# First layer: four of the six pieces of the attention's weights split ahead of the fourth chunk's inverse products, three staging buffers

## The chip, the cores and the metric

The kernel runs on one core of a Trainium2 chip. The metric is the device time of one execution in microseconds (us), lower is better. Before the change the median of 3 runs is 3002.05 us (3000.38 to 3004.14).

The engines have short names in what follows: PE multiplies matrices (PEld is its loading of weights), DVE and ACT work on vectors and single elements, POOL fills memory and issues one queue of transfers, SP issues another. Each engine takes its own instructions strictly one after another and waits for others by semaphores.

## The reference

Four layers, each added to its own input after a layer norm: a long convolution (a state space model computed by FFT), an attention with one key and value head for 32 query heads, and the same two again with the same weights. `x` is 2048 x 640.

```python
def _A_ref(u, ...):                     # convolution layer
    P = jnp.exp(logdA[:, :, None] * l[None, None, :])
    K = jnp.einsum("dn,dnl,dn->dl", Cc, P, dB).real
    Kf = rfft(pad(K)); Uf = rfft(pad(u))
    y = irfft(Uf * Kf)[..., :L]
    return y + u * Dskip

def _B_ref(x, wq, wk, wv, wo):          # attention layer
    q, k, v = x @ wq, x @ wk, x @ wv
    p = softmax(q k^T * Dh ** -0.5)
    return (p v) @ wo

x = x + _A_ref(_layernorm(x), ...)      # layer a
x = x + _B_ref(_layernorm(x), ...)      # layer b
x = x + _A_ref(_layernorm(x), ...)      # layer c
x = x + _B_ref(_layernorm(x), ...)      # layer d
```

## The kernel before

**The program.** First the convolution's kernels are generated, then come the layers a (convolution), b (attention), c (convolution), d (attention). The attention layers take most of the time. The change touches the end of layer a.

**A convolution layer** works in five chunks of 128 channels, `c` = 0 to 4. A chunk goes through these steps: the normalised input `xn` is multiplied on PE with a table `wf` (tiles `za`, L652) and ACT copies the result to a spectrum `A` (L654); DVE finishes the forward transform with short butterflies (`fft8`, L114 and L117); DVE multiplies with the spectrum of the kernel, `kh`, which SP loads (2 MB, L762, tile `Akh`); DVE does the inverse butterflies; PE multiplies with the table `wi` (`inverse`, L853 and L860, tiles `ya`) in four groups of four time steps each, and the result goes back into `x` (`residual`: by ACT on L869 for the fourth chunk, by DVE on L871 for the third and the fifth). For chunks 0 to 3 two of the products' sums are made by transfers that POOL issues and that add into `Aa` while they move (`spread`, L923 and L927). For the fifth chunk all of it is done on DVE (`product`, L837, and `fft8_last`, L157 and L160). Two banks of PSUM hold the groups of `ya` in turn, so the third group of a chunk can begin when the residual of the first has been read out.

**Statistics.** The layer norm of the attention that follows needs sums over each row of `x`. While the fourth chunk is prepared, ACT sums the channels 0 to 383, which are final by then, in four groups (`stats_first`, L692, L694, L696: four sums, one shift, four sums of squares, each writing what it doesn't need to a `dump` buffer). DVE then makes `base` of all sixteen sums of squares (`stats_base`, L701), which it needs much later.

**The attention's weights.** The attention multiplies in a format with fewer bits, in three products of high and low parts, so its weights are split once, in layer a, into `wh` (high) and `wl` (low), `attn_weights`. There are six pieces: piece 0 is `kv`, the narrow `wv` and `wk` side by side (five blocks of 20 columns each, loaded on L1017 and L1018), and pieces 1 to 5 are the five row blocks of `wq` (128 x 640 each, loaded on L1031). `first(k)` rounds a piece on ACT (L1036, into `wh`) and subtracts on PE (`ident` times the piece, L1038, plus `minus` times its high part, L1040, tile `pw`); `second(k)` copies the difference on ACT to `wl` (L1045). `scr`, the tile `xnas`, takes the place of `xn` once the fifth chunk's `za` has read it; it holds the staged row blocks, the `dump` buffers and `minus`. At the end both parts are also written to memory (`whd`, `wld`), and layer c only loads them back.

**The order.** PE, ACT and DVE follow the order in which the code is written, except that independent small instructions of DVE are moved among each other by the builder of the program; SP's and POOL's queues follow a scheduler. In the last chunk a helper, `weave`, places calls between DVE's instructions: `late` is a list of (position, call). Before the change it holds the four residuals of the fourth chunk (`turn`) and all twelve halves of the six pieces.

Of the kernel before, what the change touches and what calls it, by code (L numbers as in the profile page):

```python
# [23 lines left out]
D = 640  # L24
# [7 lines left out]
NA = D - 2 * DC  # L32
# [151 lines left out]
def weave(calls, between):  # L184

    for i in range(len(calls) + 1):
        for n, call in between:
            if n == i or (i == len(calls) and n > i):
                call()
        if i < len(calls):  # L190
            calls[i]()


class Net:
# [595 lines left out]
    def conv_layer(self, nm, first):  # L790
# [7 lines left out]
        with tc.manual_schedule(engines={mybir.EngineType.PE, mybir.EngineType.Activation,  # L798
# [29 lines left out]
            def new_xn(c):  # L828
                if "xn" in self.placed:
                    return self.placed.pop("xn")  # L830
                return cv.tile([P, 24, DC], F32, tag="xn", bufs=1, name=f"xn{nm}{c}")
# [4 lines left out]
            def product(A, kh):  # L836
                return [lambda a=a: tt(*a) for a in (  # L837
                    (m(B, 0), m(A, 0), m(kh, 0), ALU.mult),
                    (R, m(A, 1), m(kh, 1), ALU.mult),
                    (m(B, 0), m(B, 0), R, ALU.subtract),  # L840
                    (m(B, 1), m(A, 0), m(kh, 1), ALU.mult),
                    (R, m(A, 1), m(kh, 0), ALU.mult),
                    (m(B, 1), m(B, 1), R, ALU.add))]
# [22 lines left out]
            def residual(c, g, y):  # L866
                y = y.rearrange("p (t d) -> p t d", t=4)
                if c in (0, NCH - 2):
                    nc.scalar.activation(stream(c, g), y, AF.Copy)  # L869
                else:  # L870
                    tt(stream(c, g), y, stream(c, g), ALU.add)  # L871
                if c == NCH - 1:
                    self.stats_last(g)
# [65 lines left out]
            for c in range(NCH):  # L939
                A = As.pop(c)  # L940
                if c == NCH - 1:
                    late = [(1, lambda turn=turn: turn(0)), (2, lambda turn=turn: turn(1)),
                            (4, lambda turn=turn: turn(2)), (5, lambda turn=turn: turn(3))]
                    late = sorted(late + [(3 + k, a[0]) for k, a in enumerate(pieces)]
                                  + [(5 + k, a[1]) for k, a in enumerate(pieces)], key=lambda a: a[0])
                    K = khs.pop(c)
                    weave(product(A, K) + fft8_last(nc, A, B, R, K), late)
                else:
                    spread(A, khs.pop(c))
                    khs[c + 1] = self.load_spectrum(c + 1)  # L950
                    woven = [] if turn is None else [
                        (n, lambda turn=turn, g=g: turn(g)) for g, n in enumerate((2, 6, 10, 14))]
                    N = As[c + 1]
                    weave(self.whole(N, -1) if c + 1 < halved else fft8(nc, N, B, -1), woven)
                    if c + 2 < NCH:
                        As[c + 2] = prepare(c + 2)
                    if c + 2 == NCH - 1:
                        self.wfs.pop().close()
                    if c == NCH - 2:
                        scr = new_xn("s").rearrange("p a d -> p (a d)")  # L960

                        def dump(n):
                            return scr[:, 1280 + NA * (n % 4) : 1280 + NA * (n % 4) + NA]

                        self.stats_setup(nm)
                        for g in range(4):
                            self.stats_first(g, dump)
                        pieces = self.attn_weights(scr, nm == "a")
                    weave(self.whole(A, +1), ())
                ys = [inverse(c, g, K if c == NCH - 1 else A) for g in range(2)]  # L970

                def turn(g, c=c, A=A, ys=ys):

                    residual(c, g, ys[g])
                    if g < 2:
                        ys.append(inverse(c, g + 2, A))
# [24 lines left out]
    def attn_weights(self, scr, fresh):  # L1001


        nc, ins = self.nc, self.ins
        stack = ExitStack()
        wp = stack.enter_context(self.tc.tile_pool(name="wqp", bufs=1, side="right", reuse_waits="tile"))
        wh = wp.tile([P, 5, 692], F32R, name="wh")
        wl = wp.tile([P, 5, 692], F32R, name="wl")
        self.wqs = stack, wh, wl
        parts = [(w.bitcast(F32), dst) for w, dst in ((wh, self.whd), (wl, self.wld))]  # L1010
        if not fresh:
            for w, dst in parts:
                nc.sync.dma_start(w, dst.rearrange("p (k n) -> p k n", k=5))
            return []
        kv = wp.tile([P, 5, 52], F32, name="kv")
        nc.gpsimd.memset(kv, 0.0)
        nc.sync.dma_start(kv[:, :, 0:20], ins["B_wv"].rearrange("(k p) n -> p k n", p=P))  # L1017
        nc.sync.dma_start(kv[:, :, 32:52], ins["B_wk"].rearrange("(k p) n -> p k n", p=P))  # L1018
        minus = scr[:, 2816:2944]
        nc.scalar.activation(minus, self.ident, AF.Copy, scale=-1.0)  # L1020
        pws = {}

        def ends(k):
            return (wh[:, k - 1, 0:D], wl[:, k - 1, 0:D]) if k else (wh[:, :, D:692], wl[:, :, D:692])

        def first(k):
            hi = ends(k)[0]
            pw = pws[k] = self.ps2(f"pw{k}")
            if k:
                src = scr[:, D * (k % 2) : D * (k % 2) + D]  # L1030
                nc.sync.dma_start(src, ins["B_wq"][P * (k - 1) : P * k])  # L1031
                cuts = [(pw[:, a:b], src[:, a:b], hi[:, a:b]) for a, b in ((0, 512), (512, D))]
            else:
                src = kv
                cuts = [(pw[:, 0:260].rearrange("p (k n) -> p k n", k=5), src, hi)]
            nc.scalar.activation(hi, src, AF.Copy)  # L1036
            for o, a, _ in cuts:
                nc.tensor.matmul(o, self.ident, a, start=True, stop=False)  # L1038
            for o, _, b in cuts:
                nc.tensor.matmul(o, minus, b.bitcast(F32), start=False, stop=True)  # L1040

        def second(k):
            pw = pws.pop(k)
            src = pw[:, 0:D] if k else pw[:, 0:260].rearrange("p (k n) -> p k n", k=5)
            nc.scalar.activation(ends(k)[1], src, AF.Copy)  # L1045
            if k == 5:
                for w, dst in parts:
                    nc.sync.dma_start(dst.rearrange("p (k n) -> p k n", k=5), w)

        return [(lambda k=k: first(k), lambda k=k: second(k)) for k in range(6)]  # L1050

    def attn_layer(self, nm, out=None):
# [415 lines left out]
```

## Time and profile before

| what | value |
|---|---|
| median of 3 runs | 3002.05 us |
| the profiled execution's own time | 2999.59 us |
| its span, first to last instruction | 2997.8 us |
| mean granted clock of PE over the span | 0.956 |
| PE busy | 93% of the span |
| ACT busy | 81% of the span |
| DVE busy | 46% of the span |
| end of layer a, from the fifth chunk's last `za` to the attention's first product | 539.3 to 620.3 us |

The times in the rows of the trace are microseconds from the start of the span. In the view in order of time the columns are the start, the time until the group's end, the engine, the line, the operation, output and inputs, shapes, the count, and in brackets how long the engine sat idle before it and what ended that. SPq and POOLq rows are the issue of a transfer, not its landing. In the transfers' view a queue's row has packets, MB and the share of 16 transfer engines' time in the stretch asked for; q1 is the queue of SP, q0 that of POOL. In the view by stretches a row has the stretch, its length, the busy time of PE, PEld, DVE, ACT and POOL with counts, PE's granted clock (1.00 is full), the transfer engines' share and GB/s. Some of the instructions of the program appear as two in the trace of PE: one product of `inverse` is two there.

### The profile page before, as it was taken

Reading aid. Unit: us, or ns where it says so; the run is one execution under the profiler, and the core shown is the slowest. Engines: PE = TensorE matmul, PEld = TensorE weight load, DVE = VectorE, ACT = ScalarE, POOL = GpSimd, SP = SyncE. Lnnn points to the kernel's source line nnn. Section 1 sums busy time; section 2 is a strip of 40 time slices with the busy share of each in tenths; the row PEclk is TensorE's granted clock in tenths of the full one; section 3 lists DMA queues with packets and bytes.
Section 4 is the critical chain, followed back from the end, with each engine's and each line's share of the span. In section 5 each row is a group of like instructions: output and inputs, shape, how many; then the busy total and the mean of one; then the engine's idle time right before and its main releaser. Section 6 shows DMA issues by size and latency. Waiting matters only on the chain. (4 is left out here: it accounts for less than half of the span.)

```text
span 2997.8 us, 52536 instructions
## 1 busy us (share of the span) xinstructions
PE 2777.6 (93%) x21712; PEld 1269.2 (42%) x21712; DVE 1378.1 (46%) x1794; ACT 2426.4 (81%) x2904; POOL 86.7 (3%) x149
## 2 busy tenths in 40 slices
PE   2776989898999999999999998898999999999999
PEld 0333978775232333232333687772233333333333
DVE  7999899942122332322232599722222322222222
ACT  5888243444999999999999634338999999999997
POOL 0001001000000000000000011000000000000000
PEclk9855999999999999999999999899999999999999
DMA  6113555433200000001000256131001101110100
GB/s 145 34 19 100 186 162 113 104 114 113 81 22 25 22 25 22 27 21 28 21 26 20 87 113 160 39 129 51 22 25 26 39 21 28 38 26 24 41 19 23
DMA packets 126000, 175.60 MB, mean 59 GB/s; under 512 B 59460, under 2 KB 81988, under 8 KB 122132
## 3 DMA queue, kind: packets, MB, share of 16 engines
q1 hardware_dynamic: 102680, 137.70, 15.8%
q0 software_dynamic: 21104, 33.45, 5.5%
q8 instruction: 175, 2.87, 0.4%
q10 hardware_dynamic: 1968, 0.98, 0.1%
q14 instruction: 73, 0.60, 0.1%
HBM read 95.22 MB, written 48.04 MB: 48 GB/s over the span
## 5 line engine op out<-in xcount | busy, mean ns | idle before, releaser
L1264 ACT ACTIVATE pt<-scb 128x1024 f32<-128x1024 f32 x1024 | 942.2, 1113 | 6.7 <-PE scb L1260 5.1
L1264 ACT ACTIVATE pt<-scd 128x1024 f32<-128x1024 f32 x1024 | 942.1, 1115 | 5.8 <-DMA qpd<-mxd 3.9
L1274 PE MATMUL pob<-pt,vt 128*32 128x512 f32 x4096 | 546.6, 606 | 4.4 <-DVE on L1291 0.2
L1274 PE MATMUL pod<-pt,vt 128*32 128x512 f32 x4096 | 546.3, 605 | 4.4 <-DVE on L1291 0.2
L1260 PE MATMUL scb<-qpb,kt 62*128 62x512 f32 x2048 | 385.8, 451 | 6.0 <-DVEq L1209 5.6
L1260 PE MATMUL scd<-qpd,kt 62*128 62x512 f32 x2048 | 385.4, 451 | 5.6 <-DVEq L1209 5.2
L1260 PEld LDWEIGHTS scb<-qpb,kt 62*128 62x128 f32 x2048 | 166.0, 185 | 401.4 <-ACT pt L1264 392.0
L1260 PEld LDWEIGHTS scd<-qpd,kt 62*128 62x128 f32 x2048 | 165.8, 184 | 401.1 <-ACT pt L1264 392.2
L1322 DVE TENSOR_TENSOR x<-pyd,x 128x320 f32<-128x320 f32 x146 | 71.8, 491 | 560.9 <-PE pyd L1334 560.9
L1322 DVE TENSOR_TENSOR x<-pyb,x 128x320 f32<-128x320 f32 x146 | 71.8, 492 | 547.4 <-PE pyb L1334 547.4
L1294 DVE RECIPROCAL rc<-rc 128x512 f32<-128x512 f32 x62 | 207.9, 3353 | 2.1
L1274 PEld LDWEIGHTS pob<-pt,vt 128*32 128x32 f32 x4096 | 80.6, 108 | 178.1 <-issue 160.0
L1274 PEld LDWEIGHTS pod<-pt,vt 128*32 128x32 f32 x4096 | 80.6, 108 | 177.6 <-issue 159.5
L1334 PE MATMUL pyb<-wo,ot 128*32 128x320 f32 x1168 | 105.3, 432 | 0.0
L1334 PE MATMUL pyd<-wo,ot 128*32 128x320 f32 x1168 | 105.3, 432 | 0.0
L652 PE MATMUL za<-xna,wf 128*128 128x256 f32 x384 | 87.4, 390 | 5.0 <-ACT xna L818 5.0
L652 PE MATMUL zc<-xnc,wf 128*128 128x256 f32 x384 | 85.8, 385 | 5.0 <-ACT xnc L818 5.0
L860 PE MATMUL ya<-Aa,wi 128*128 128x128 f32 x576 | 71.8, 289 | 15.5 <-DVE Aa L114 15.5
L1291 DVE COPY on<-pod 128x512 f32<-128x512 f32 x31 | 21.4, 691 | 134.6 <-PE pod L1274 120.6
L1291 DVE COPY on<-pob 128x512 f32<-128x512 f32 x31 | 21.4, 691 | 133.0 <-PE pob L1274 110.0
L443 PE MATMUL pe<-kg,tm 48*128 48x512 bf16 (+1 forms) x120 | 60.1, 603 | 23.9 <-ACT m L451 15.4
L652 PEld LDWEIGHTS za<-xna,wf 128*128 128x128 f32 x384 | 74.8, 196 | 16.8 <-ACT xna L818 6.2
(367 smaller groups left out, 3204.2 us busy)
## 6 DMA issues: line engine op xcount, KB each, us to landing
Akh<-kh SPq DMA_DIRECT2D x10, 2048.0 KB
kh<-Ak SPq DMA_DIRECT2D x5, 2048.0 KB
qhd<-qh SPq DMA_DIRECT2D x40, 256.0 KB
qld<-ql SPq DMA_DIRECT2D x40, 256.0 KB
qpb<-qhd SPq DMA_DIRECT2D x256, 40.0 KB
qpd<-qhd SPq DMA_DIRECT2D x256, 40.0 KB
ot<-on SPq DMA_DIRECT2D x216, 40.0 KB
wf<-in_c_wf POOLq DMA_DIRECT2D x16, 512.0 KB, 7.9
```

Of the source, the lines that this page charges most:

```text
L443: nc.tensor.matmul(pe[:, 512 * h : 512 * h + 512], grp(tm, u, par, rows), kg[0:rows, col : col + 512], start=True, stop=True)
L652: nc.tensor.matmul(zv[:, :, c, kk], self.wf[:, t + 4 * h, j, c, kk], x, start=(n == 0), stop=(n == 3))
L860: nc.tensor.matmul(y[:, s * DC : (s + 1) * DC], self.wi[:, t, j, c_, kk], v[:, 2 * t + c_, kk], start=(i == 0 and not whole), stop=(i == 3 ...
L1260: nc.tensor.matmul(sc[:, 512 * par : 512 * par + 512], kt[rows, 128 * t : 128 * t + 128], qps[nb, hg, pr][rows], start=True, stop=True)
L1264: nc.scalar.activation(pt, sc, AF.Exp, scale=SCALE)
L1274: nc.tensor.matmul(po[32 * j : 32 * j + 32], vt[:, t], pts[step, j // 2][:, 512 * (j % 2) : 512 * (j % 2) + 512], start=(t == 0), stop=(t ...
L1291: nc.vector.tensor_copy(on, po)
L1294: nc.vector.reciprocal(rc, rc)
L1322: nc.vector.tensor_tensor(xh, py, xh, ALU.add)
L1334: nc.tensor.matmul(py[j : j + m], o[:, 128 * i + j : 128 * i + j + m], w[:, 320 * half : 320 * half + 320], start=start, stop=stop)
```

## The change

Four of the six pieces are begun ahead of the statistics of the fourth chunk instead of being woven into the fifth: `first` of pieces 0 to 3 stands before `stats_first(0)`, `second(0)` after `stats_first(1)`, `second(1)` after `stats_first(2)`, `second(2)` and `second(3)` after `stats_first(3)`. Pieces 4 and 5 stay in the fifth chunk, behind its residuals. The staged row blocks get three buffers in place of two, the `dump` buffers two in place of four, and `minus` moves. The program of layer c has the same two `dump` buffers, and nothing else of the change.

```diff
@@ -941,8 +941,8 @@
                 if c == NCH - 1:
                     late = [(1, lambda turn=turn: turn(0)), (2, lambda turn=turn: turn(1)),
                             (4, lambda turn=turn: turn(2)), (5, lambda turn=turn: turn(3))]
-                    late = sorted(late + [(3 + k, a[0]) for k, a in enumerate(pieces)]
-                                  + [(5 + k, a[1]) for k, a in enumerate(pieces)], key=lambda a: a[0])
+                    late = sorted(late + [(6 + k, a[0]) for k, a in enumerate(pieces[4:])]
+                                  + [(8 + k, a[1]) for k, a in enumerate(pieces[4:])], key=lambda a: a[0])
                     K = khs.pop(c)
                     weave(product(A, K) + fft8_last(nc, A, B, R, K), late)
                 else:
@@ -960,12 +960,16 @@
                         scr = new_xn("s").rearrange("p a d -> p (a d)")
 
                         def dump(n):
-                            return scr[:, 1280 + NA * (n % 4) : 1280 + NA * (n % 4) + NA]
+                            return scr[:, 1920 + NA * (n % 2) : 1920 + NA * (n % 2) + NA]
 
                         self.stats_setup(nm)
+                        pieces = self.attn_weights(scr, first)
+                        for a in pieces[:4]:
+                            a[0]()
                         for g in range(4):
                             self.stats_first(g, dump)
-                        pieces = self.attn_weights(scr, nm == "a")
+                            for a in pieces[max(g - 1, 0) : (0, 1, 2, 4)[g]]:
+                                a[1]()
                     weave(self.whole(A, +1), ())
                 ys = [inverse(c, g, K if c == NCH - 1 else A) for g in range(2)]
 
@@ -1016,7 +1020,7 @@
         nc.gpsimd.memset(kv, 0.0)
         nc.sync.dma_start(kv[:, :, 0:20], ins["B_wv"].rearrange("(k p) n -> p k n", p=P))
         nc.sync.dma_start(kv[:, :, 32:52], ins["B_wk"].rearrange("(k p) n -> p k n", p=P))
-        minus = scr[:, 2816:2944]
+        minus = scr[:, 2688:2816]
         nc.scalar.activation(minus, self.ident, AF.Copy, scale=-1.0)
         pws = {}
 
@@ -1027,7 +1031,7 @@
             hi = ends(k)[0]
             pw = pws[k] = self.ps2(f"pw{k}")
             if k:
-                src = scr[:, D * (k % 2) : D * (k % 2) + D]
+                src = scr[:, D * (k % 3) : D * (k % 3) + D]
                 nc.sync.dma_start(src, ins["B_wq"][P * (k - 1) : P * k])
                 cuts = [(pw[:, a:b], src[:, a:b], hi[:, a:b]) for a, b in ((0, 512), (512, D))]
             else:
```

Behind the inserted code the lines of the changed kernel are higher by 4: L1036 is L1040 there. Three places of the engines' orders matter below.

ACT, after its last copy of the fifth chunk's `za`: a row with + stands there now, the others stood there before (`wh` is the high part, `xnas` the staged row blocks, `L692` the first statistics).

```order
 L654 ACTIVATE Aa_3955<-za_2_3992 128x2x512
 L654 ACTIVATE Aa_3955<-za_3_4010 128x2x512
+L1024 ACTIVATE xnas<-ident 128x128
+L1040 ACTIVATE wh<-kv 128x5x52
+L1040 ACTIVATE wh<-xnas 128x640 x3
 L692 ACTIVATE xnas,smsuma<-x 128x384 x4
 L694 ACTIVATE smshifta<-smsuma 128x4
```

So `minus` and the rounding of four pieces now stand ahead of the first statistics, and what they wait for the statistics wait for too.

DVE, in the inverse butterflies of the fourth chunk (`Aa_3737`): a row with - stood there before, with + it stands there now.

```order
 L114 TENSOR_TENSOR Aa_3737<-B 128x512 x2
-L701 TENSOR_SCALAR smbasea<-smsqa 128x16
 L114 TENSOR_TENSOR B<-Aa_3737 128x512 x2
 L114 TENSOR_TENSOR Aa_3737<-B 128x2x256 x2
 L114 TENSOR_TENSOR B<-B 128x2x256 x2
+L701 TENSOR_SCALAR smbasea<-smsqa 128x16
 L117 SCALAR_TENSOR_TENSOR Aa_3737<-B 128x512 x2
 L117 SCALAR_TENSOR_TENSOR Aa_3737<-B 128x2x256 x2
```

`stats_base`, which reads the sums of squares of all four groups, moves back by six instructions, but it still stands ahead of the last butterflies of the fourth chunk and of everything of the fifth.

SP, in the queue of the changed kernel from the load of the fourth chunk's kernel spectrum (`Akh_3874`) to that of the whole split weights.

```order
L762 DMA Akh_3874<-kh 128x4096
L1035 DMA xnas<-in_B_wq 128x640 x2
L1021 DMA kv<-in_B_wv 128x5x20
L1022 DMA kv<-in_B_wk 128x5x20
L1035 DMA xnas<-in_B_wq 128x640
L762 DMA Akh_4093<-kh 128x4096
L1035 DMA xnas<-in_B_wq 128x640 x2
L1052 DMA whd<-wh 128x3460
```

One load of a row block has moved from behind the fifth chunk's spectrum (`Akh_4093`), where three stood, to ahead of it; the two loads of `kv` stand where they stood.

## The prediction

> **What bounds the kernel now.** I read the page first, then the trace from 539 to 620 us in order of time, engine by engine, because the edit lies inside layer a alone; the attention layers, most of the time, only shift with it. On PE:
>
> ```profile
> 564.58 6.76 PE L860 MATMUL ya<-Aa,wi 128*128 128x128 f32 x32 [9.98 <-DVE Aa L114]
> ...
> 580.90 3.73 PE L860 MATMUL ya<-Aa,wi 128*128 128x128 f32 x32
> 584.47 0.60 PE L1038 MATMUL pw<-kv,ident 128*128 128x260 f32 x2
> ...
> 591.91 1.25 PE L1038 MATMUL pw<-xnas,ident 128*128 128x512 f32 x4
> ...
> 596.30 7.31 PE L860 MATMUL ya<-Akh,wi 128*128 128x128 f32 x64
> 603.45 7.31 PE L860 MATMUL ya<-Aa,wi 128*128 128x128 f32 x64
> ...
> 620.26 0.43 PE L1131 MATMUL pqb<-xh,wh 128*52 128x512 f32 x1 [1.35 <-DVE xl L999]
> ```
>
> From 564.58 to 610.76 (603.45 + 7.31) only the first row has an idle time: PE never stops. It does the fourth chunk's four groups, from 584.47 to 596.3 all six pieces, then the fifth chunk's four groups. Ahead of that it stood idle for 9.98 us, which the change wants to fill. DVE over the same time:
>
> ```profile
> 565.05 0.17 DVE L701 TENSOR_SCALAR smbasea<-smsqa 128x16 f32<-128x16 f32 x1
> 565.16 1.29 DVE L114 TENSOR_TENSOR B<-Aa 128x512 f32<-128x512 f32 x2
> ...
> 568.89 2.50 DVE L117 SCALAR_TENSOR_TENSOR Aa<-B 128x512 f32<-128x512 f32 x4
> 571.43 2.29 DVE L837 TENSOR_TENSOR B<-Aa,Akh 128x2048 f32<-128x2048 f32 x1
> ...
> 589.61 2.49 DVE L157 TENSOR_TENSOR Akh<-Ra 128x512 f32<-128x512 f32 x4
> ```
>
> No row has an idle time: DVE is a chain without gaps. Its first quarter of the output that the fifth chunk's first group reads is ready at 589.61 + 0.62 = 590.2, but PE takes it up at 596.30. So over the last stretch the six pieces on PE decide, by 6.1 us; before it, DVE does. Both bounds lie close together, so a gain on PE is capped by DVE.
>
> **What the removal is worth.** Four pieces leave the tail: from 584.47 to 591.91 is 7.44 us of PE, about 2.2 for a wide piece. DVE's cap makes it less, and layer c shows the capped case: the same chain with no pieces.
>
> ```profile
> 1876.83 2.29 DVE L837 TENSOR_TENSOR B<-Ac,Akh 128x2048 f32<-128x2048 f32 x1
> ...
> 1904.71 2.48 DVE L160 SCALAR_TENSOR_TENSOR Ac<-B 128x512 f32<-128x512 f32 x4
> ```
> ```profile
> 1895.81 10.30 PE L860 MATMUL yc<-Akh,wi 128*128 128x128 f32 x64 [6.49 <-issue]
> 1905.94 7.31 PE L860 MATMUL yc<-Ac,wi 128*128 128x128 f32 x64
> ...
> 1923.07 0.43 PE L1131 MATMUL pqd<-xh,wh 128*52 128x512 f32 x1 [1.09 <-DVE xl L999]
> ```
>
> From DVE's first fifth-chunk product to the attention's first product layer c takes 1923.07 - 1876.83 = 46.24 us, layer a 620.26 - 571.43 = 48.83. The removal is worth 2.6 us, not 7.4. Part of what is lost is PE's clock: the 64 instructions take 10.30 us there against 7.31, after 6.49 us of idling.
>
> ```profile
> 1892.00:1895.00 3.00, 0.00 (x0) 0.00 (x0) 2.97 (x3) 0.00 (x0) 0.00 (x0) 0.50 0.00 0
> ```
>
> The clock column stands at half here, 2.7 us into that gap. In the changed kernel my estimate of the gap is 4.4 us (below), so I take layer c's number. If PE stayed at full clock, the second half could begin when DVE's first L160 result is there (1904.71 + 0.62 = 1905.33 instead of 1905.94), some 0.6 to 0.9 us earlier with DVE's own wait for PE gone: the removal is worth 2.6 to 3.5. [...]
>
> **What the new place costs.** ACT before:
>
> ```profile
> 543.85 0.52 ACT L692 ACTIVATE xnas<-x 128x384 f32<-128x384 f32 x1 [3.33 <-DVE x L871]
> ...
> 562.96 0.19 ACT L696 ACTIVATION_READ_ACCUMULATOR xnas<-x,smshifta 128x1 f32 x1
> 563.06 0.29 ACT L1020 ACTIVATE xnas<-ident 128x128 f32<-128x128 f32 x1
> ```
>
> The statistics take 563.06 - 543.85 = 19.2 us of ACT without a gap and end 1.9 us ahead of L701, the one DVE instruction that reads them all. Now the rounding of pieces 0 to 3 stands ahead of them, and its first piece is `kv`. When does `kv` land? Nobody waited for it before, so I read SP's queue and the bytes, q1 in 544 to 548 us and in 548 to 553.5 us, then both queues in 549 to 550:
>
> ```profile
> 539.53 1.44 SPq L1031 DMA_DIRECT2D xnas<-in_B_wq  x2
> 541.22 1.31 SPq L1017 DMA_DIRECT2D kv<-in_B_wv  x1
> 542.58 1.87 SPq L1018 DMA_DIRECT2D kv<-in_B_wk  x1
> 553.54 0.34 SPq L762 DMA_DIRECT2D Akh<-kh  x1
> ```
> ```profile
> q1 hardware_dynamic: 278, 0.64, 45.8%
> ```
> ```profile
> q1 hardware_dynamic: 1322, 0.12, 30.6%
> ```
> ```profile
> q0 software_dynamic: 189, 0.19, 116.0%
> q1 hardware_dynamic: 190, 0.02, 30.2%
> ```
>
> The first 0.64 MB are the two row blocks (2 x 320 KB). The next 1322 packets with 0.12 MB can only be `kv`: 2 x 128 x 5 = 1280 rows of 80 bytes. They crawl, taking turns packet for packet (190 against 189) with POOL's adding transfers, and the last of them moves in the quarter of a microsecond from 553.25:
>
> ```profile
> q1 hardware_dynamic: 12, 0.00, 3.5%
> ```
>
> What lies between data and use I take from the first late row block: its issue, its last data (q1 in the tenth of a microsecond from 589.1), its use on ACT.
>
> ```profile
> 586.65 4.73 SPq L1031 DMA_DIRECT2D xnas<-in_B_wq  x3
> ```
> ```profile
> q1 hardware_dynamic: 2, 0.00, 1.1%
> ```
> ```profile
> 576.30 0.41 ACT L1036 ACTIVATE wh<-kv 128x260 fp32r<-128x260 f32 x1
> ...
> 585.16 0.73 ACT L1036 ACTIVATE wh<-xnas 128x640 fp32r<-128x640 f32 x1
> 585.79 0.38 ACT L1045 ACTIVATE wl<-pw 128x260 fp32r<-128x260 f32 x1
> ...
> 589.56 0.74 ACT L1036 ACTIVATE wh<-xnas 128x640 fp32r<-128x640 f32 x1 [3.39 <-DMA xnas<-in_B_wq]
> ...
> 594.60 1.28 ACT L1045 ACTIVATE wl<-pw 128x640 fp32r<-128x640 f32 x2
> ```
>
> From 589.1 to 589.56 are 0.4 us. So ACT rounds `kv` at 553.4 + 0.4 = 553.8. Start to start `kv` takes 0.31 us (0.41 less the overlap of 0.1) and a row block 0.63 (585.16 to 585.79): 0.3 + 3 x 0.63 = 2.2. The statistics begin at 556.0, not 543.85.
>
> The third row block, now third in the queue behind `kv`, is needed at 555.3. It must follow `kv` on the transfer engines. At best it costs nothing; at worst it takes, from 553.4 on, all that the late row block took from issue (586.65) to use, 2.9 us, and lands 1.0 late. I take 0, since its issue is long past and only about 1.5 us of moving is left, and keep 1.0 for the range. `minus` (0.29) fits into the wait.
>
> From 556.0 the statistics run 19.2 us, with `second(0)` (0.28) and `second(1)` (0.59, half of 1.28 less the overlap) between them; PE has both differences by 558, long before ACT asks. End: 556.0 + 19.2 + 0.9 = 576.1, with the last read-out 576.2. DVE comes to L701 in its new place at 568.89 - 0.11 = 568.8. **It waits 7.4 us there.** Behind L701 are queued the last butterflies of the fourth chunk and the whole fifth chunk, all that PE waits for at the end. Before, this wait was zero with 1.9 us to spare.
>
> The other edits cost nothing as long as that wait covers them. PE's fourth difference needs a tile that `second(0)` frees at 565.9, and at half clock it takes twice 2.2 us, to 570.3; the fourth chunk's first group then ends near 575.5. The four residuals on ACT follow the statistics and `second(2)`, `second(3)` from 577.3. PE's groups and the last two pieces (2 x 2.2) end near 593.2; DVE's first output comes at 590.2 + 7.4 = 597.6, which is the gap of 4.4 us. The spectrum of the fifth chunk, issued at 553.54, follows 320 KB that now move first, about 1 us; it is used at 578.8. Two `dump` buffers in place of four: a write waits for the write two before it on its own engine, which has ended; nothing (rival B prices the other case). Layer c: nothing.
>
> **The sum**, on the profiled execution: 2999.59 + 7.4 (DVE waits) - 2.6 (pieces out of the tail) = 3004.4. The median of the runs shown lies 2.46 above that execution, so 3002.05 + 4.8 = **3006.9 us**.
>
> **The rivals.**
>
> A, the forecast. Bounds from its own terms: 7.4 to 8.4 for the wait, 2.6 to 3.5 for the gain, so +3.9 to +5.8; with the scatter of the runs (3000.38 to 3004.14, 2 us to either side of the median) +2 to +8.
>
> B, the wait is longer still, because each statistic waits for the one just before it to write its `dump` buffer.
>
> ```profile
> 545.38 0.51 ACT L692 ACTIVATE xnas<-x 128x384 f32<-128x384 f32 x1
> 545.80 0.19 ACT L692 ACTIVATION_READ_ACCUMULATOR xnas<-x 128x1 f32 x1
> 546.02 0.20 ACT L694 ACTIVATE smshifta<-smsuma 128x4 f32<-128x4 f32 x1
> ```
>
> L694 waits for the sum before it and starts 0.64 after that sum's start, where sums follow one another by 0.5. For the 24 statistics that aren't first of their four, 24 x 0.14 = 3.4 more: +8.2, 3010.2. Against it: two buffers call for the write two back only.
>
> C, the other side: `kv` lands early and nothing is slower. It would take that its 1280 rows don't wait for POOL's transfers. If they need only their own share (30.6% of 5.5 us = 1.7), they are done by 549.7, the wait shrinks by 3.7 and the sum is +1.1, 3003.2. For the wait to vanish, `kv` must be usable by 553.8 - 7.4 = 546.4; then only the gain stays: 2999.5 on the median. For it: `kv` is issued by 544.45, and a late block took 2.9 us from issue to use. Against it: the counted packets of this very stretch, with the same queues ahead. [...]
>
> D, PE's chain becomes late. Its groups wait for the residuals, which now stand behind the statistics; if half clock lasted through all four groups (3.7 us each at full), 4 x 3.7 = 15 us more would put PE's last piece at 608, 10 past DVE's output, and the sum at +15. The point from which it decides is 4.4 us of lateness. Against it: in this place before only the first group ran slow, 6.76 us for 32 instructions against 3.73 later. I price the likely partial case at +4 on top, +8.8, 3010.9.
>
> **How the numbers follow.** About 0.2% (6.0 us) is what a measurement of this kernel can tell from no change. A 0.62, of which 0.25 above +6.0 (late third block, scatter) and 0.37 below; B 0.18; D 0.09; C 0.11, of which 0.03 beyond -6.0 with scatter. Slower 0.25 + 0.18 + 0.09 = 0.52, same 0.37 + 0.08 = 0.45, faster 0.03. Range: from A's lower end less the better part of C's first case, 3002.0, to past B and D, 3011.5.
>
> **What would show it.** Right: ACT's first `wh` row waits until near 553.8 for `kv`; the first L692 near 556; L701 with an idle time of some 7 us put down to ACT; the first L837 near 578.8; PE idle 4 to 5 us ahead of `ya<-Akh`, and half clock behind it; the attention's first product near 625. Wrong: an L692 before 550, or L701 with no idle time (C), sums 0.64 apart (B), or `ya<-Akh` starting directly behind the pieces (D). An unchanged stretch of 46.2 us from L837 on with another total would mean the time went elsewhere.

## The result, and the profile after

| what | before | changed |
|---|---|---|
| median, beside each other (14 runs each) | 3001.10 us (2997.40 to 3004.14) | 3008.73 us (3004.84 to 3009.79) |
| ratio of the times, 95% interval | 1 | 1.0023 (1.0016 to 1.0030) |
| the profiled execution's own time, its span | 2999.59, 2997.8 us | 3006.02, 3004.2 us |
| mean granted clock of PE over the span | 0.956 | 0.951 |
| fifth chunk's last forward product to the attention's first product, layer a | 81.2 us | 85.5 us |
| the same in layer c | 80.9 us | 80.5 us |
| first projection of the attention, layer b | 100.8 us | 102.5 us |
| the same projection in layer d | 100.8 us | 102.4 us |

The change costs 7.6 us, between 4.8 and 9.0. The last four rows are differences of starts and ends in the trace of each kernel and hold whatever came ahead of them; that matters here, because this execution of the changed kernel reached the end of the fifth chunk's forward products 2.5 us earlier than that of before (536.6 against 539.1 us). Of the 6.4 us between the two profiled executions the place of the edit holds +4.3, the two projections +1.7 and +1.6, the stretch in layer c -0.4, and the rest, of either sign, lies in the long stretches between.

ACT of the changed kernel, in order of time:

```profile
551.33 0.42 ACT L1040 ACTIVATE wh<-kv 128x260 fp32r<-128x260 f32 x1 [13.14 <-DMA kv<-in_B_wk]
551.65 1.98 ACT L1040 ACTIVATE wh<-xnas 128x640 fp32r<-128x640 f32 x3
553.53 0.51 ACT L692 ACTIVATE xnas<-x 128x384 f32<-128x384 f32 x1
553.95 0.19 ACT L692 ACTIVATION_READ_ACCUMULATOR xnas<-x 128x1 f32 x1
554.04 0.51 ACT L692 ACTIVATE xnas<-x 128x384 f32<-128x384 f32 x1
```

ACT stands still for 13.14 us for the rows of `kv`, which come 14.7 us after the fifth chunk's last forward product. The three row blocks behind it have no wait of their own. Then the statistics run, one sum every 0.5 us. DVE of the same kernel:

```profile
565.05 1.28 DVE L114 TENSOR_TENSOR B<-B 128x512 f32<-128x512 f32 x2
573.70 0.17 DVE L701 TENSOR_SCALAR smbasea<-smsqa 128x16 f32<-128x16 f32 x1 [7.36 <-ACT xnas L696]
573.78 2.49 DVE L117 SCALAR_TENSOR_TENSOR Aa<-B 128x512 f32<-128x512 f32 x4
576.31 2.29 DVE L837 TENSOR_TENSOR B<-Aa,Akh 128x2048 f32<-128x2048 f32 x1
```

The chain that had no idle time before has one now, 7.36 us, put down to ACT's last sum of squares. The instruction that waits works for 0.17 us, but the fifth chunk is queued behind it. PE, which waits for that chunk:

```profile
563.54 2.50 PE L1042 MATMUL pw<-xnas,ident 128*128 128x512 f32 x4 [6.71 <-ACT wl L1049]
...
589.41 1.25 PE L1044 MATMUL pw<-wh,xnas 128*128 128x512 f32 x4
595.28 8.98 PE L860 MATMUL ya<-Akh,wi 128*128 128x128 f32 x64 [4.63 <-issue]
604.59 7.39 PE L860 MATMUL ya<-Aa,wi 128*128 128x128 f32 x64 [0.33 <-DVE Aa L160]
...
616.80 4.23 PE L1118 MATMUL ptb<-ident,x 128*128 128x128 f32 x17 [3.21 <-ACT x L1109]
622.13 0.67 PE L1135 MATMUL pqb<-xh,wh 128*52 128x512 f32 x1 [1.09 <-DVE xl L1003]
622.59 0.63 PE L1135 MATMUL pqb<-xh,wl 128*52 128x512 f32 x1
```

The pieces are out of the tail: PE is done with the last one at 590.7 and then idles for 4.63 us, where before it ran through. The group behind the gap takes 8.98 us instead of 7.31, at a lower clock (the columns are those of the view by stretches; the clock stands third from the right):

```profile
591.80:595.21 3.41, 0.00 (x0) 0.00 (x0) 3.38 (x5) 0.00 (x0) 0.00 (x0) 1.00 0.94 398
595.21:598.62 3.41, 3.34 (x16) 3.37 (x17) 3.41 (x4) 0.00 (x0) 0.00 (x0) 0.50 0.46 195
```

The clock fell as the gap ended, not within it. New, and nowhere in the prediction, is the last row pair of PE: the attention's first products take 0.63 us each instead of 0.40, and they start 0.43 us apart instead of 0.23.

### The profile page after: what moved, and what is told of

Its sections match the earlier page's. It is cut to its first block, busy times and chain, and to the rows that moved or that the text cites. A ratio compares the mean times of both kernels' runs of the same rounds, so it can differ in the third digit from the quotient of the medians.

```text
span 3004.2 us, 52536 instructions
## 1 busy us (share of the span) xinstructions
PE 2782.4 (93%) x21712; PEld 1266.6 (42%) x21712; DVE 1376.7 (46%) x1794; ACT 2426.0 (81%) x2904; POOL 86.6 (3%) x149
## 5 line engine op out<-in xcount | busy, mean ns | idle before, releaser
L1278 PEld LDWEIGHTS pod<-pt,vt 128*32 128x32 f32 x4096 | 80.6, 108 | 178.1 <-issue 160.1
L1278 PEld LDWEIGHTS pob<-pt,vt 128*32 128x32 f32 x4096 | 80.6, 108 | 178.0 <-issue 160.0
L652 PEld LDWEIGHTS zc<-xnc,wf 128*128 128x128 f32 x384 | 73.7, 193 | 16.4 <-ACT xnc L818 6.2
```

The lines of the kernel that those rows point to most:

```text
L652: nc.tensor.matmul(zv[:, :, c, kk], self.wf[:, t + 4 * h, j, c, kk], x, start=(n == 0), stop=(n == 3))
L1278: nc.tensor.matmul(po[32 * j : 32 * j + 32], vt[:, t], pts[step, j // 2][:, 512 * (j % 2) : 512 * (j % 2) + 512], start=(t == 0), stop=(t ...
```

## The experiments

One table first, all in us. "Stretch" is that from the fifth chunk's last forward product to the attention's first product; the next two columns are the first projections of layers b and d. The first four kernels ran beside the kernel before at 3001.57, the next four at 3000.89, the last three at 3000.61.

| run | median | ratio (95%) | stretch | b | d | idle ahead of the base |
|---|---|---|---|---|---|---|
| before, as profiled | 3001.10 | 1 | 81.2 | 100.8 | 100.8 | 0 |
| changed, as profiled | 3008.73 | 1.0023 (1.0016 to 1.0030) | 85.5 | 102.5 | 102.4 | 7.36 |
| e1 changed again (one run) | 3008.47 | - | 85.6 | 102.6 | 102.5 | 7.31 |
| e2 base on POOL | 3001.62 | 1.0000 (0.9991 to 1.0009) | 78.3 | 102.9 | 102.5 | gone |
| e3 buffers alone | 3002.11 | 1.0005 (0.9996 to 1.0014) | 81.0 | 100.7 | 102.5 | 0 |
| e4 `kv` loaded early | 3001.72 | 1.0000 (0.9991 to 1.0009) | 80.9 | 100.8 | 102.3 | 2.64 |
| e5 before, PE kept busy | 2998.40 | 0.9994 (0.9985 to 1.0003) | 80.6 | 100.9 | 100.8 | 0 |
| e6 changed, PE kept busy | 3001.94 | 1.0005 (0.9996 to 1.0014) | 84.9 | 100.9 | 100.9 | 7.31 |
| e7 `kv` early, base on POOL | 2997.06 | 0.9989 (0.9980 to 0.9998) | 78.2 | 100.8 | 100.7 | gone |
| e8 as e7, PE kept busy | 2994.70 | 0.9980 (0.9971 to 0.9989) | 77.6 | 100.7 | 100.7 | gone |
| e9 before, PE busy, `kv` alone ahead | 3005.15 | 1.0014 (1.0005 to 1.0023) | 87.0 | 100.7 | 100.9 | 8.30 |
| e10 `kv` late, base on POOL, PE busy | 2994.66 | 0.9982 (0.9973 to 0.9991) | 78.9 | 100.8 | 100.8 | gone |
| e11 e8 again | 2994.84 | 0.9981 (0.9972 to 0.9990) | 77.6 | 100.7 | 100.7 | gone |

**e1, the changed kernel again.** No edit.

> The changed kernel once more, for a second profile. Theory T (DVE waits at L701 for the statistics on ACT, which wait for the landing of kv): ACT idles about 13 us ahead of its first wh row, L701 shows an idle time of 7.0 to 7.8 us, and from DVE's first L837 row to the attention's first product are 45.8 to 46.3 us. The clock behind the attention's first product (half for 3.9 us in the first profile) is a matter of phase by T and may be full here; by rival R2 (the time is lost elsewhere: clock, buffers, layer c) it is half again.

The wait, the stretch and the longer projections came again, each within 0.1 us of the first profile.

**e2, the base on POOL.** The waiting instruction leaves DVE's queue; ACT still waits for `kv`.

```diff
-    def stats_base(self):
-        nc, sm = self.nc, self.sm
-        nc.vector.tensor_scalar(sm["base"], sm["sq"], 1.0 / D, EPS, ALU.mult, ALU.add)
+    def stats_base(self, eng):
+        sm = self.sm
+        eng.tensor_scalar(sm["base"], sm["sq"], 1.0 / D, EPS, ALU.mult, ALU.add)
...
-        self.stats_base()
+        self.stats_base(nc.gpsimd if first else nc.vector)
```

> The changed kernel with the base of layer a (L701) made on POOL, so that DVE no longer waits for the statistics; ACT still does all it did. T: DVE's wait of 7.4 us goes, PE's chain of the fourth chunk and the last two pieces (ends 593.2 on the time axis of before) becomes the bound in place of 596.3, so 2.9 us faster than before: about 2998, 10 us below the changed kernel. Rival R1 (what costs is PE's own chain, whose groups wait for residuals queued behind the statistics on ACT): no change, about 3008. R2: about 3008.

ACT, then DVE, of this kernel:

```profile
553.94 0.42 ACT L1040 ACTIVATE wh<-kv 128x260 fp32r<-128x260 f32 x1 [13.12 <-DMA kv<-in_B_wk]
```
```profile
567.68 1.29 DVE L114 TENSOR_TENSOR B<-B 128x512 f32<-128x512 f32 x2
569.01 2.50 DVE L117 SCALAR_TENSOR_TENSOR Aa<-B 128x512 f32<-128x512 f32 x4
571.54 2.29 DVE L837 TENSOR_TENSOR B<-Aa,Akh 128x2048 f32<-128x2048 f32 x1
```

ACT waits as long as before, 13.12 us, and DVE not at all. The stretch is 78.3 us: 7.2 below the changed kernel and 2.9 below the kernel before, the wait and the gain one by one. So what costs time is not that ACT waits but that one short instruction on DVE waits for ACT. The median is that of the kernel before (3001.62 beside 3001.57) and not the 2998 that was expected: the projections of this profile are the longer ones, by 2.1 and 1.7 us against before, more in sum than the local 2.9.

**e3, the buffers alone.** The two `dump` buffers, the three staging buffers and the place of `minus` on the kernel before, in the old order.

```diff
-                            return scr[:, 1280 + NA * (n % 4) : 1280 + NA * (n % 4) + NA]
+                            return scr[:, 1920 + NA * (n % 2) : 1920 + NA * (n % 2) + NA]
...
-                src = scr[:, D * (k % 2) : D * (k % 2) + D]
+                src = scr[:, D * (k % 3) : D * (k % 3) + D]
```

> The kernel before with the change's buffers alone: two dump buffers, three staged row blocks, minus moved; the pieces stay where they were. T and R1: no change, within 1 us of before, L701 without idle time. R2, or each statistic waiting for the one before it: 3 us or more above before.

No change in time or stretch: the buffers have no part in the cost at the edit. The projection in layer d is the longer one here too, 102.5 us; since e7 has the same two buffers in layer c and 100.7, the buffers alone don't make it longer.

**e4, `kv` loaded ahead of the first layer**, into a tile of its own; the rest is the changed kernel.

```diff
+        self.kv = self.xp.tile([P, 5, 52], F32, name="kv")
...
+        nc.gpsimd.memset(self.kv, 0.0)
+        nc.sync.dma_start(self.kv[:, :, 0:20], self.ins["B_wv"].rearrange("(k p) n -> p k n", p=P))
+        nc.sync.dma_start(self.kv[:, :, 32:52], self.ins["B_wk"].rearrange("(k p) n -> p k n", p=P))
...
-        kv = wp.tile([P, 5, 52], F32, name="kv")
-        nc.gpsimd.memset(kv, 0.0)
-        nc.sync.dma_start(kv[:, :, 0:20], ins["B_wv"].rearrange("(k p) n -> p k n", p=P))
-        nc.sync.dma_start(kv[:, :, 32:52], ins["B_wk"].rearrange("(k p) n -> p k n", p=P))
+        kv = self.kv
```

> The changed kernel with kv loaded at the start of the program, next to x, into a tile of its own. T: ACT rounds kv at once and waits only for the third row block, which no longer queues behind kv and can be used near 550.2 on the time axis of before; statistics from 550.8, end at 571.0, L701 waits about 2.2 us in place of 7.4; with the gain of 2.6 about 0.4 us faster than before (2999.5 to 3002). R1 and R2: 3006 or more, since the pieces stand where the change put them.

ACT, then DVE, of this kernel (its lines are higher by one on ACT, by four in the statistics):

```profile
542.28 0.41 ACT L1041 ACTIVATE wh<-kv 128x260 fp32r<-128x260 f32 x1
549.05 0.74 ACT L1041 ACTIVATE wh<-xnas 128x640 fp32r<-128x640 f32 x1 [6.36 <-DMA xnas<-in_B_wq]
550.70 0.74 ACT L1041 ACTIVATE wh<-xnas 128x640 fp32r<-128x640 f32 x1 [0.91 <-DMA xnas<-in_B_wq]
552.33 0.74 ACT L1041 ACTIVATE wh<-xnas 128x640 fp32r<-128x640 f32 x1 [0.89 <-DMA xnas<-in_B_wq]
```
```profile
573.18 0.17 DVE L705 TENSOR_SCALAR smbasea<-smsqa 128x16 f32<-128x16 f32 x1 [2.64 <-ACT xnas L700]
```

The wait for `kv` is gone and a wait for the wide row blocks takes part of its place: 2.64 us at the base, 2.2 expected. That is about what the pieces' removal brings, and the stretch comes out 0.3 below that of before.

**e5 and e6, PE kept busy.** Fourteen matmuls into a spare PSUM tile stand behind the last inverse product of layers a and c, in the kernel before (e5) and in the changed one (e6); they read the last residual, so they run in PE's pause ahead of the attention's transposes, and nothing reads what they write.

```diff
         for g in range(1, 4):
             turn(g)
+        w = self.ps2(f"warm{nm}")
+        for i in range(14):
+            nc.tensor.matmul(w[:, DC * (i % 8) : DC * (i % 8) + DC], self.ident, self.x[:, TAUS[12], 4 * DC : 5 * DC], start=True, stop=True)
         self.norm_part(1, 3)
```

> The kernel before, with 14 matmuls of 128x128 into a spare PSUM tile behind the last inverse product of layers a and c; they read the last residual of the fifth chunk, so they run in TensorE's pause before the transposes of the attention's input. Nothing reads their result. Theory (the attention's first products run at half clock for some 4 us whenever that pause lets the clock fall at a bad moment; in the profile of the kernel before this happened in neither layer, in three of four later profiles of other kernels it happened in layer d): the length of the attention's projection from its first to its last product is 100.8 us in both layers (as in the profile of before), never 102.5; time within 1.5 us of the kernel before, that is 3000 to 3001.6, since its executions already have the full clock in layer b. Rival (the half clock is noise that follows nothing in this pause): some projection is still 102.5 us long. Second rival (the dummies only delay the transposes): first product later by their 1.6 us, 3002 to 3004.

> The changed kernel, with the same 14 matmuls behind the last inverse product of layers a and c. Theory (of the +7.4 us measured, +4.4 are the wait at L701 less the gain, and 1.7 to 2.1 in layer b are the half clock of the first products): projection of layer b 100.8 us instead of 102.5, the stretch from the fifth chunk's forward products to the first product still 85.5 us, time about 3007 less another 1.6 if layer d also lost its full clock in the runs of the changed kernel: 3005 to 3007.2. Rival (the longer projection comes from the pieces' moved weights, or from a transfer): it stays at 102.5 and the time at 3008.5. Second rival (half clock falls at random): the profile shows 102.5 in one of the layers all the same.

PE of e6, to be laid beside the rows from 616.80 on of the changed kernel above:

```profile
614.78 3.39 PE L989 MATMUL warma<-x,ident 128*128 128x128 f32 x28 [1.42 <-DVE x L871]
618.01 1.52 PE L1121 MATMUL ptb<-ident,x 128*128 128x128 f32 x9
619.79 1.42 PE L1121 MATMUL ptb<-ident,x 128*128 128x128 f32 x11 [0.26 <-ACT x L1112]
622.93 0.43 PE L1138 MATMUL pqb<-xh,wh 128*52 128x512 f32 x1 [1.72 <-DVE xl L1006]
623.20 0.40 PE L1138 MATMUL pqb<-xh,wl 128*52 128x512 f32 x1
```

All four projections of the two runs are 100.8 to 100.9 us long, so the longer ones were a matter of PE's clock, which is 1.00 from 609.0 to 619.2 us in e5 and from 613.0 to 626.6 us in e6, and of nothing that the change moved into them. The transposes, faster as well (20 of them in 3.20 us in e6, where 17 take 4.23 in the changed kernel), bring the first product forward: in layer a by 0.6 us in both kernels (81.2 to 80.6, and 85.5 to 84.9), in layer c by 1.7 us in the kernel before (80.9 to 79.2) and by 1.3 us in the changed one (80.5 to 79.2). With the clock out of the way the change costs 3001.94 - 2998.40 = 3.5 us, near the local +4.3. Both times lie under what was expected (3000 to 3001.6, and 3005 to 3007.2).

In e5 the two stretches make 2.3 of the 2.5 us by which it lies below the kernel before (3000.89), so this gain doesn't call for any clock lost in that kernel's projections; the interval of its ratio still holds 1. For e6, the times beside the kernel before went from +7.6 to +1.0, by 6.6 us; the two projections (1.6 and 1.5) and the two stretches (0.6 and 1.3) are 5.0 of that. The other 1.6 us are less than the two intervals leave open.

**e7, `kv` early and the base on POOL** (the edits of e4 and e2 on the changed kernel), **and e8, the same with PE kept busy.**

> The changed kernel with the value and key weights loaded before the first layer into a tile of their own, and the first statistics' base on GpSimd, so that VectorE waits neither for ACT nor computes L701. Theory (each edit removes the whole wait by itself; together they add up to no more than the gain of the removal, VectorE being the bound of that stretch): the stretch to the first product 77.5 to 78.5 us (81.2 before, 78.3 with the base on GpSimd alone), so 3.0 to 3.7 us less than before, of which up to 1.7 per attention layer can be lost to the clock: 2997.5 to 3001.5. Rival (the tail is bound by the chain of residuals and statistics, no longer by the forwarded product): the stretch stays at 78.3 or above and nothing is gained over the base on GpSimd alone: 3001 to 3002.

> The kernel of the run with early value and key weights and the base on GpSimd, with the 14 matmuls behind the last inverse product of layers a and c as well. Theory (stretch to the first product 77.5 to 78.5 us, projections 100.8 us in layers b and d): 3.0 to 3.7 us less than before with no clock lost: 2996.5 to 2998.5, faster than both kernels. Rival (the half clock follows nothing in that pause): 2998 to 3001.5, as without the dummies.

e7's stretch, 78.2 us, is that of e2 within the 0.1 that profiles differ by: the base on POOL removes the whole of DVE's wait, and the early load, which by itself leaves 2.64 us of it (e4), adds nothing to that. This lies in the theory's range and 0.1 from the bound that the rival named, so the stretch doesn't part the two. Its time, 2997.06, lies just below the expected range; in its profile both projections are at full clock without the matmuls, 3.9 us less in sum than e2's. e8 has a stretch of 77.6 and lies below both kernels, by 0.20% (0.11 to 0.29) against before; it too lies lower than expected (2996.5 to 2998.5). Of the 2.4 us between e7 and e8, whose intervals overlap, the stretches of layers a and c are 2.0 (0.6, and 80.9 to 79.5).

**e9, the suspected cost alone.** The kernel of e5 with one step of the change, `first(0)` ahead of the statistics: the high half of `kv` on ACT and, with it, that piece's difference on PE (0.9 us). Its copy to `wl` and the five wide pieces stay where they were.

```diff
+                        pieces = self.attn_weights(scr, nm == "a")
+                        if pieces:
+                            pieces[0][0]()
+                            pieces[0] = (lambda: None, pieces[0][1])
                         for g in range(4):
                             self.stats_first(g, dump)
-                        pieces = self.attn_weights(scr, nm == "a")
```

> The kernel before with the 14 matmuls (so that the clock takes no part), and with one step of the change alone: only the first high half of the value and key piece, with its wait for the rows, is issued ahead of the statistics; all six pieces still end in the last product. Theory (the wait of ACT for the rows is the whole cost, and the pieces' way out of the tail the whole gain): in this order VectorE reaches L701 25.9 us after the fifth chunk's forward products, as before; the rows land 14.7 us after them, and one copy and the 19.2 us of statistics follow, so L701 waits until 34.3: some 8.4 us, with no more than 0.5 us of gain against it. Stretch to the first product 80.6 (with these matmuls, without the edit) + 8 = 88 to 89 us; time 2998.4 + 8 = 3006 to 3007, more than the whole change costs with these matmuls (+3.5). Rival (the cost is the four pieces' matmuls and splits in PE's and ACT's order, not the wait): no change, stretch 80 to 81, 2998 to 2999.

DVE, then PE, of this kernel:

```profile
573.85 0.17 DVE L701 TENSOR_SCALAR smbasea<-smsqa 128x16 f32<-128x16 f32 x1 [8.30 <-ACT xnas L696]
...
580.19 2.29 DVE L837 TENSOR_TENSOR B<-Aa,Akh 128x2048 f32<-128x2048 f32 x1
...
598.38 2.49 DVE L157 TENSOR_TENSOR Akh<-Ra 128x512 f32<-128x512 f32 x4
```
```profile
598.66 1.25 PE L1046 MATMUL pw<-wh,xnas 128*128 128x512 f32 x4
599.75 7.31 PE L860 MATMUL ya<-Akh,wi 128*128 128x128 f32 x64
610.12 7.41 PE L860 MATMUL ya<-Aa,wi 128*128 128x128 f32 x64 [3.06 <-DVE x L871]
...
626.47 0.43 PE L1137 MATMUL pqb<-xh,wh 128*52 128x512 f32 x1 [1.72 <-DVE xl L1005]
```

A copy of 0.42 us, moved with what belongs to it, costs 3005.15 - 2998.40 = 6.8 us (the two ran beside the kernel before at 3000.61 and 3000.89), nearly twice what the whole change costs under the same matmuls; 3006 to 3007 was expected. The wait is 8.30 us (8.4 expected), but only 87.0 - 80.6 = 6.4 of it reach the first product: the stretch was expected at 88 to 89. The rows say why: the five wide pieces stand in the tail as before, and yet L837 to the first product is 46.28 us, against 48.2 in e5 (570.29 to 618.53). While DVE stood still, PE went on. At `ya<-Akh` it is now 0.8 us behind DVE's first output (599.75 against 598.38 + 0.62), where it is 6.0 us behind in e5 (595.14 against 588.48 + 0.62); of that the narrow piece's difference is 0.9. Then DVE is the late one, PE waits 3.06 us for it, and at the first product 1.9 us of the gain are left.

**e10, another way to the same end.** `kv` is loaded and split in the fifth chunk, pieces 1 to 3 stay ahead, the base is on POOL and PE is kept busy: no tile is needed ahead of the first layer.

```diff
-                    late = sorted(late + [(6 + k, a[0]) for k, a in enumerate(pieces[4:])]
-                                  + [(8 + k, a[1]) for k, a in enumerate(pieces[4:])], key=lambda a: a[0])
+                    late = sorted(late + [(6 + k, a[0]) for k, a in enumerate(pieces[:1] + pieces[4:])]
+                                  + [(8 + k, a[1]) for k, a in enumerate(pieces[:1] + pieces[4:])], key=lambda a: a[0])
...
-                        for a in pieces[:4]:
+                        for a in pieces[1:4]:
```

> The changed kernel with the 14 matmuls, the base on GpSimd, and three pieces ahead instead of four: the value and key piece, whose rows are late, is loaded and split in the last product, so no tile for it is needed before the first layer. Theory: VectorE waits for nothing, three of the pieces are out of the tail: the stretch to the first product 77.6 us as in the run with early value and key weights (VectorE bounds it), 78.2 at most with the two or three more splits in the tail; 2994.5 to 2996. Rival (each piece in the tail costs): 79 us or more, 2996 or more.

The time is that of e8 and as expected; the stretch, 78.9 us, is 1.3 longer than in e8, above the theory's 78.2 and 0.1 below the rival's 79. PE of this kernel:

```profile
587.57 1.25 PE L1047 MATMUL pw<-wh,xnas 128*128 128x512 f32 x4
588.65 7.31 PE L860 MATMUL ya<-Akh,wi 128*128 128x128 f32 x64
598.12 9.01 PE L860 MATMUL ya<-Aa,wi 128*128 128x128 f32 x64 [2.16 <-DVE Aa L160]
```

The pieces hold PE up by 0.3 us at most: it takes up the fifth chunk at 588.65, and DVE's first output is there at 588.4. Later PE waits 2.16 us for DVE, and the 64 instructions behind that take 9.01 us instead of 7.31 (the clock was 0.50 from 599.6 to 603.0). The time doesn't show the 1.3, so between the two theories this run decides nothing.

**e11, e8 again.**

> The fastest of the kernels so far again, with early value and key weights, the base on GpSimd and the 14 matmuls: 2994.7 within 1.5 us, stretch 77.6, projections 100.7.

2994.84 against 2994.70: the gain stands.

## Why the prediction was right, point by point

**The wait.** 7.4 us were predicted, 7.36 and 7.31 measured, and each link of the chain came out as worked out: `kv` used 14.7 us after the last forward product (14.7 predicted: 553.8 against 539.1), no wait for the third row block (0 taken, 1.0 kept for the range), the statistics 2.2 us after `kv`, `second(0)` and `second(1)` between them. e2, e4 and e9 show that this wait is the cost: it goes with the instruction, shrinks with the load, and comes with `first(0)` alone.

**The gain of the removal**, 2.6 us. L837 to the first product is 576.31 to 622.13, 45.82 us, against 48.83: 3.0, inside the 2.6 to 3.5. e2 gets 2.9 with no wait at all. What the prediction didn't see is whose gain it was in the changed kernel: e9 gets 1.9 of it with no more than the narrow piece's difference (0.9 us of PE) out of the tail. It is the distance by which PE's chain ends behind DVE's, which goes if the pieces leave and is used up if DVE is late. The sum holds, since it was made from DVE's side (the capped stretch of layer c), but in the changed kernel the pieces' early place is worth, by a comparison of two kernels, only about the rest: 46.28 in e9 against 45.26 in e6 (577.67 to 622.93), 1.0 us.

**The sum**, +4.8 us, measured +4.3 and +4.4 in the place of the edit. On the whole program it was too small: 3008.73 where 3006.9 was forecast, +7.6 (4.8 to 9.0) beside the kernel before, outside the +3.9 to +5.8 of A's own terms and inside its +2 to +8 with the scatter. The term that was missing, and so stood at nothing without a reason, is PE's clock behind the edit. The prediction looked at the clock in the 4.4 us gap ahead of `ya<-Akh`, where it fell only as the gap ended (595.2), and ended its sum at the attention's first product; the first 3.8 us behind that (622.13 to 625.93) run at half clock in the changed kernel, which is 1.7 us in layer b, and 1.6 in layer d, where the program differs by nothing but the two `dump` buffers. e6 takes both away. That the time lies in the range, 3002.0 to 3011.5, and that the change came out above +6.0, is in part luck: the range was made wide for scatter and for rivals that didn't come, and A's share above +6.0 was given to a late third block and to scatter, not to the clock.

**The rivals.** B (statistics wait for each other) is refuted by sums 0.5 us apart in the changed kernel and by e3. C (`kv` lands early) is refuted by the 13.14 us; e4 makes its case by hand and lands at -0.3 rather than C's -2.6, since the wide row blocks then take over a part of the wait. The prediction's "taking turns packet for packet" is more than its counts, 190 against 189, show: equal counts would also come of larger groups, if those of both queues are alike. D (PE's chain late) is refuted by the 4.63 us for which PE has nothing to do.

**What was to show it** showed it: the first `wh` row after 13 us of idling, the first L692 at 553.53 (556.0 less the 2.5 us by which this execution was ahead), L701's idle time put down to ACT, PE's gap of 4.63 with a slow group behind it.

## What to carry to other kernels

Before work is moved into an idle stretch of an in-order engine, look up when its input lands and then follow the queue to the last reader on every other engine: the price was set by an instruction of 0.17 us on a third engine, two steps from the edit. If two engines' chains end close together, a delay on one and a relief of the other are not independent terms; try the delay alone. And where an engine's clock follows its work, end a sum behind the first burst after a pause, not ahead of it: some matmuls that nobody reads, in a pause of 4 us, went with 2.4 to 6.6 us less out of 3000 here, of which only the 6.6 of the changed kernel are clear of the intervals.

## What the runs showed of the hardware

**The granted clock changes in steps of 3.41 us.** The traces keep a record of the clock that PE was granted. In all thirteen it is 1.00 or 0.50 and nothing between, and every stretch at one clock, but for the last of each trace, is a whole number of steps of 3.413 us (from 1 to 303 of them in the traces of the two kernels). Some of these steps, first in the changed kernel, from the end of layer a on (columns: stretch, length, busy time of PE, PEld, DVE, ACT and POOL with counts, PE's clock, transfer share, GB/s):

```profile
612.30:615.71 3.41, 0.55 (x3) 0.31 (x3) 3.32 (x19) 0.69 (x1) 0.00 (x0) 1.00 0.00 0
615.71:619.12 3.41, 2.32 (x9) 1.70 (x10) 1.36 (x7) 2.65 (x4) 0.00 (x0) 0.50 0.00 0
619.12:622.54 3.42, 2.33 (x10) 1.76 (x10) 1.69 (x2) 2.71 (x4) 0.00 (x0) 0.50 0.00 0
622.54:625.95 3.41, 3.41 (x9) 1.62 (x8) 1.26 (x2) 3.06 (x4) 0.00 (x0) 0.50 0.00 0
625.95:629.30 3.35, 3.35 (x16) 2.39 (x15) 0.63 (x1) 1.07 (x2) 0.00 (x0) 1.00 0.00 0
```

The same in the kernel before, from the end of layer a and, last two rows, of layer c:

```profile
611.70:615.10 3.40, 0.71 (x4) 0.48 (x5) 2.95 (x18) 1.31 (x4) 0.00 (x0) 1.00 0.00 0
615.10:618.51 3.41, 3.39 (x15) 2.68 (x15) 0.49 (x3) 1.99 (x3) 0.00 (x0) 0.50 0.00 0
618.51:621.93 3.42, 2.07 (x12) 1.09 (x11) 2.95 (x3) 3.42 (x6) 0.00 (x0) 1.00 0.00 0
...
1912.16:1915.57 3.41, 1.64 (x13) 1.21 (x12) 3.38 (x14) 0.92 (x1) 0.00 (x0) 1.00 0.02 5
1915.57:1918.99 3.42, 1.25 (x5) 0.94 (x6) 2.38 (x17) 2.33 (x4) 0.00 (x0) 0.50 0.00 0
```

In both, a step in which PE is busy for 0.55 or 0.71 us, and in layer c even 1.64, is followed by half clock. At the end of layer a the kernel before fills the next step (3.39 us) and has its clock back ahead of the first product at 620.26. The changed kernel fills only 2.32 and 2.33 of the next two, because its transposes begin 1.1 us into the first of them and the pause ahead of the product lies in the second; the third is filled by products at half speed. In e2 one step with 2.97 us of work was not enough for the clock to come back, and in e7 one with 2.92 was:

```profile
611.73:615.15 3.42, 2.97 (x13) 2.35 (x14) 1.01 (x6) 2.02 (x3) 0.00 (x0) 0.50 0.00 0
615.15:618.55 3.40, 2.31 (x9) 1.46 (x9) 2.32 (x3) 3.33 (x5) 0.00 (x0) 0.50 0.00 0
618.55:621.95 3.40, 3.40 (x10) 1.61 (x9) 0.63 (x2) 2.44 (x4) 0.00 (x0) 0.50 0.00 0
```
```profile
1914.58:1917.99 3.41, 2.92 (x14) 2.21 (x11) 0.50 (x1) 1.95 (x3) 0.00 (x0) 0.50 0.00 0
1917.99:1921.41 3.42, 2.64 (x12) 1.46 (x13) 2.45 (x3) 3.42 (x6) 0.00 (x0) 1.00 0.00 0
```

So PE's busy time, as the trace models it, doesn't tell to a tenth of a microsecond when the clock comes back. When it falls is clearer: from 300 us on the thirteen traces hold 144 falls, each behind a step with at most 1.69 us of work on PE, half of its length, and of some 9800 steps at full clock with no fall behind them only seven had less than 1.70 us (the least 1.48). The kernel before has 12 of the falls, behind 0 to 1.64 us of work, the changed one 13, behind 0 to 1.58; each has 750 of the other steps and none of the seven. With the 14 matmuls of e6 the stretches of 3.4 us from 613.0, 616.4 and 619.8 us hold 1.98, 3.04 and 1.68 us of work, and the clock stays at 1.00. How much work a step gets depends on where its edges fall in a pause, and with it whether the next burst pays nothing (projections of 100.7 to 100.9 us) or 1.4 to 2.2 us (102.3 to 102.9). In the rows of this section the clock fell after steps that were not idle: PE was busy for 0.55 to 1.64 us of them, a sixth to a half of their length. The changed kernel had half clock in its first products in both layers of both its profiles, the kernel before, in its one profile, in neither. Whether the order of the change makes this more likely, or the steps happened to lie so, the runs don't settle: e3, in the order of before, had it in layer d, and e7, in the order of the change, in neither. With the 14 matmuls it is in neither layer of e5, e6, e8, e9, e10 and e11 (100.7 to 100.9 us).

**Rows of 80 bytes go through in equal numbers with another queue's rows of about 1 KB**, in the changed kernel as before (189 against 190 there in the microsecond from 549 us). Its transfers in the microsecond from 547 us (q0 is POOL's queue, q1 SP's):

```profile
q0 software_dynamic: 186, 0.18, 114.6%
q1 hardware_dynamic: 185, 0.01, 29.5%
```

0.01 MB goes through in the time of 0.18 MB. Whether single rows take turns or small groups, these counts over all transfer engines don't show. So `kv`, the smallest piece with its 1280 rows, is the last of the first four pieces that ACT has to wait for; no run without POOL's transfers was made, so that they hold it up is argued from the counts.
